# Short convolution on quarters of the TensorE array's rows, with a new written-out order, in a fused long-convolution and SwiGLU block

## The chip, the cores and the metric

The kernel runs on one core of a Trainium2 chip. The metric is the device time of one execution in microseconds (us); less is better. "The trace" is one execution recorded by the hardware profiler, "the profile" the page made from it. Engines: PE is TensorE (PEld its weight loads), DVE is VectorE, ACT is ScalarE, POOL is GpSimd, SP is SyncE, here only a queue that issues DMAs.

## The reference, cut to what matters

Sequence S = 2048, width D = 640, FFN width 1728, all bfloat16.

```python
x = A_q
n = layernorm(x)
kshift[t] = sum over i in 0..3 of k[t-i] * shift_k[:, i]     # short convolution, four taps per channel
kv = kshift * v
y = causal long convolution of kv with ssm_k (length 2048), by FFT
y = y + kv * ssm_D
h = x + n * y
out = h + (silu(layernorm(h) @ w_gate) * (layernorm(h) @ w_up)) @ w_down
```

## The kernel before, in words

**Blocks and stages.** The sequence is cut into NB = 4 blocks of 512 tokens. Token t of a block sits in partition t // 4, row r = t % 4, so a block is a tile of 128 partitions by 4 x 640. The FFT is done by matmuls with constant cosine and sine tables: `WF` forward and `WI` back, both loaded from HBM. For each block j there are these stages, in the names that the planner gives them:

- `k`: k is turned so that channels lie on partitions, in the tile `T` (block 0 by PE transposes, blocks 1 to 3 by transposing DMAs in `load_rows`). The short convolution runs on PE in `by_halves` (line 745), and ACT or DVE take the result out of PSUM and multiply it by v (lines 763, 764, 766). That gives kv.
- `X` and `G`: spectra of kv and of the filter (`spectrum`, `transform`, `forward`: matmuls on line 400, evictions on lines 389 and 392). `g_turned` first turns the filter block, by PE transposes (line 498) and evictions (line 500), or, for blocks in `GTURN`, by one ACT copy (line 484) and four transposing DMAs (line 488).
- `h` and `m`: DVE combines filter spectra of two blocks and multiplies and adds spectra (lines 544 to 567, 865, 893, 894). Block j needs j + 1 products. Some of the additions are given to DMAs that add into SBUF (line 292).
- `i`: the inverse transform (DVE sums on lines 979 to 1016, matmuls on line 1036), then for each of four rows the gate `n * y`, its row sum and the residual (`h1`, lines 1060 and 1074; block 0 on lines 1047 and 1050), then squares for the second layernorm (ACT, line 905) and the normalisation.
- `t`: the normalised rows are scaled (lines 960, 963) and turned, block 0 by PE (lines 1096, 1098), the others by four transposing DMAs (line 1089).
- `f`: the FFN of the block, 135 matmuls of 512 columns (line 1260) and 112 of the down projection (line 1153), with ACT and DVE between.

So block j's FFN can start when its `t` stage is complete; block j + 1's `k` to `t` stages run beside block j's FFN. What comes before the FFN of block 0 is called the prologue below.

**Sums in the spectrum.** `transform` makes a spectrum from sums over even and odd rows. In the way called "sub" each of four output groups takes two accumulations of four matmuls (two rows, two column halves), and DVE makes the upper half with one subtraction of 128 x 2560. In the way called "four" (listed in `SUM`) it uses a further symmetry: half of the matmuls, the same number of evictions, and on DVE two differences of 128 x 1280 (line 464) and two sums of 128 x 2560 (lines 468, 471).

**Short convolution.** `pairs` holds, for each tap and each group of 128 channels, a diagonal matrix folded to 64 columns, built once on DVE (line 1424). A matmul takes 64 of the array's 128 rows: the weights are a window of `T` (64 channels by 128 tokens), the moving operand up to four taps by 64 columns. The two halves of the rows write to two PSUM banks. The five channel groups are done in three goes of 2, 2 and 1, each with one PSUM slot of two banks.

**Order.** A planner, `Plan`, numbers every piece of work (`plan.add`) with the engine it runs on, the buffers it needs and an assumed duration. `schedule` then emits the pieces in the order of the list `ORDER`, so this list fixes the sequence on every engine and DMA queue. A negative number picks a piece's alternative: DVE instead of ACT, a POOL-issued DMA instead of one from SP, or an adding DMA instead of a DVE addition. The assumed durations are used only to make the list; at run time the engines wait on semaphores. There are four PSUM slots (`ps`) of two banks each, shared by all stages, and 13 SBUF slots (`big`).

At the start PE multiplies ones (`spin`, line 1410, counts in `WARMUP` and `SPINS`) so that its clock is up, while the first loads come in.

Of the kernel before, what the change touches and what calls it, by code (L numbers as in the profile page):

```python
# [44 lines left out]
GTURN = (3,)  # L45
KTURN = (1, 2, 3)
SUM = {'X2': 'four', 'X3': 'four', 'i2': 'four', 'i3': 'four', 'G3': 'four'}
# [3 lines left out]
WARMUP = (18, 16, 16)  # L51
SPINS = (2, 2)
MERGE = ()
WIDE = ()
H1ACT = ()
# [17 lines left out]
TAPROWS = True  # L73
TWONS = 640
# [146 lines left out]
def kernel(ctx: ExitStack, tc: tile.TileContext, A_q, A_k, A_v, A_shift_k, A_ssm_k, A_ssm_D, B_x,  # L221
# [93 lines left out]
    if TAPROWS:  # L315
        T = fixed([P, KT * TW], BF16, "T")
        ident2 = fixed([P, P // 2], BF16, "ident2")
        pairs = fixed([P, 4 * KT, P // 2], BF16, "pairs")

        def tk():  # L320
            return ap(T).rearrange("p (c t) -> p c t", c=KT)

        def tk0():
            return ap(T)[:, 0:KT * R * (P + 1)].rearrange("p (c r t) -> p c r t", c=KT, r=R)
        TOKENS = tuple((a, r) for a in range(R) for r in range(R))
    else:
        diag = new("diag") if TWOTAPS else fixed([P, KT * 4, P], BF16, "diag")
# [342 lines left out]
    def kv_of(j, kT, before, v, behind=None):  # L670

        if TAPROWS:
            if j == 0:
                dve(60, lambda: nc.vector.memset(tk0()[:, :, :, 0:1], 0.0), [], [of_t("K0")])
            kv = new("t4")
            by_halves(j, kv, v, behind)
            return kv
# [932 lines left out]
```

## Time and profile before

| | |
|---|---|
| median of 3 runs | 255.96 us (255.7 to 256.19) |
| the profiled execution | 256.9 us, of which the span of instructions is 254.8 us |
| PE busy | 247.1 us, 97% of the span |
| DVE busy | 193.7 us, 76% |
| ACT busy | 171.0 us, 67% |
| POOL busy | 61.2 us, 24% |
| granted TensorE clock | 1.0 |
| DMA | 42.80 MB, mean 168 GB/s |

The profiled execution took 0.9 us more than the median. Busy time of PE counts overlapping matmuls as busy throughout, so its share is read together with the chain of waits: the list of instructions, followed back from the last one, of which each released the next.

### The profile page before, as it was taken

What the parts mean: (1) busy time and instruction counts of PE and PEld (TensorE: products, weight loads), DVE (VectorE), ACT (ScalarE), POOL (GpSimd) and SP (SyncE); (2) the same over time, 40 slices, a digit from 0 to 9 for tenths busy, and PEclk for the clock granted to TensorE, in tenths of its full rate; (3) what the DMA queues carried; (4) which work ended last, traced back from release to release, by engine and by line L of the source; (5) the groups of instructions that cost most, each with busy time, mean ns of one, the idle gap of its engine ahead of it and who ended that gap; (6) DMA issues with size and microseconds to landing.
All of it is one profiled execution on the core that took longest, in us unless ns stands there. A gap on an engine that the chain in (4) does not pass through costs nothing.

```text
span 254.8 us, 4493 instructions
## 1 busy us (share of the span) xinstructions
PE 247.1 (97%) x1758; PEld 146.8 (58%) x1758; DVE 193.7 (76%) x256; ACT 171.0 (67%) x295; POOL 61.2 (24%) x72
## 2 busy tenths in 40 slices
PE   8889999999999999999999999999999999999995
PEld 8756776644445776654564576544447754444663
DVE  0879999999999999999999999999999100020322
ACT  2789989987989964877796965645697244653400
POOL 2203240012560400541415203309900042000000
PEclk9999999999999999999999999999999999999999
DMA  5999999999996797999977877997770476000003
GB/s 183 391 345 152 371 287 219 330 190 174 166 256 135 174 155 168 192 223 176 289 170 104 207 134 166 253 195 124 152 215 1 93 103 115 0 3 0 0 0 105
DMA packets 54591, 42.80 MB, mean 168 GB/s; under 512 B 25557, under 2 KB 48730, under 8 KB 54570
## 3 DMA queue, kind: packets, MB, share of 16 engines
q1 hardware_dynamic: 47664, 28.25, 44.3%
q0 software_dynamic: 6896, 14.26, 30.6%
q8 instruction: 14, 0.23, 0.4%
q14 instruction: 7, 0.06, 0.1%
q10 hardware_dynamic: 10, 0.01, 0.0%
HBM read 23.99 MB, written 4.59 MB: 112 GB/s over the span
## 4 chain that ended last, share of the span: by engine, by line
PE 83%; ACT 7%; DMA 4%; DVE 2%; SPq 1%; issue 1%; DVEq 0%
PE ps L1260 46%; PE ps L1153 24%; PE ps L400 6%; DMA WF<-const_wf 4%; PE ps L1036 4%; PE ps L745 3%; ACT big L389 3%; ACT S L389 2%; DVE big L1050 1%; ACT big L500 1%; ACT big L1098 1%; ACT row L905 1%; DVE row L1047 1%; SPq L362 0%; PE ps L498 0%
## 5 line engine op out<-in xcount | busy, mean ns | idle before, releaser
L1260 PE MATMUL ps<-big,big 128*128 128x512 bf16 x540 | 119.4, 379 | 0.0
L1260 PEld LDWEIGHTS <-big 128*128 128x128 bf16 x540 | 52.7, 98 | 61.1 <-issue 0.2
L1153 PE MATMUL ps<-wd,tT 128*128 128x320 bf16 (+2 forms) x416 | 58.4, 299 | 0.0
L1153 PEld LDWEIGHTS <-tT 128*128 128x128 bf16 x416 | 40.1, 98 | 17.0 <-issue 1.3
L400 PE MATMUL ps<-big,WF 128*128 128x320 bf16 x224 | 35.9, 298 | 3.2 <-DMA WF<-const_wf 1.6
L1252 ACT ACTIVATE tT<-ps 128x1024 bf16<-128x1024 f32 x24 | 24.5, 1023 | 17.5 <-PE ps L1260 17.4
L893 DVE TENSOR_TENSOR big<-S,S 128x2560 bf16<-128x2560 bf16 x24 | 34.9, 1487 | 0.1
L1254 DVE TENSOR_TENSOR tT<-tT,co 128x2048 bf16<-128x2048 bf16 x12 | 14.6, 1222 | 25.0 <-ACT co L1250 25.0
L1250 ACT CAST co<-ps 128x1024 bf16<-128x1024 f32 x24 | 23.9, 1012 | 12.8 <-PE ps L1260 11.3
L400 PEld LDWEIGHTS <-WF 128*128 128x128 bf16 x224 | 21.5, 97 | 14.6 <-issue 3.5
L292 POOL DMA_DIRECT2D S<-big x13 | 15.2, 1173 | 55.7 <-DVE big L865 24.7
L894 DVE TENSOR_TENSOR S<-S,big 128x2560 bf16<-128x2560 bf16 x16 | 23.7, 1487 | 0.1
L905 ACT ACTIVATE row<-big 128x640 bf16<-128x640 bf16 x32 | 23.5, 735 | 0.5 <-DVE big L1050 0.2
L963 ACT ACTIVATE row<-big,sm 128x640 bf16<-128x640 bf16 x20 | 17.7, 921 | 6.8 <-DVE sm L941 6.8
L1189 POOL DMA_DIRECT2D out_dram<-row x12 | 13.1, 1231 | 22.4 <-ACT row L1188 22.1
L389 ACT ACTIVATE big<-ps 128x640 bf16<-128x640 f32 (+1 forms) x29 | 16.8, 625 | 0.9 <-PE ps L400 0.9
L1188 ACT CAST row<-ps 128x640 bf16<-128x640 f32 x12 | 7.7, 699 | 13.8 <-PE ps L1153 12.3
L389 ACT CAST S<-ps 128x640 bf16<-128x640 f32 (+1 forms) x26 | 14.7, 623 | 1.1 <-PE ps L400 1.1
L952 ACT ACTIVATE row<-big 128x640 bf16<-128x640 bf16 x16 | 11.9, 741 | 1.4 <-DMA big<-in_A_q_dram 1.4
L865 DVE TENSOR_TENSOR S<-S,S 128x2560 bf16<-128x2560 bf16 (+1 forms) x10 | 12.1, 1220 | 0.0
L865 DVE TENSOR_TENSOR big<-S,S 128x2560 bf16<-128x2560 bf16 (+1 forms) x10 | 12.0, 1220 | 0.0
L1036 PEld LDWEIGHTS <-WI 128*128 128x128 bf16 x96 | 9.2, 98 | 4.8 <-issue 0.2
(99 smaller groups left out, 265.0 us busy)
## 6 DMA issues: line engine op xcount, KB each, us to landing
S<-big POOLq DMA_DIRECT2D x11, 640.0 KB, 6.2
big<-in_B_w_gate_dram SPq DMA_DIRECT2D x13, 320.0 KB, 5.6
big<-in_B_w_up_dram SPq DMA_DIRECT2D x12, 320.0 KB, 6.2
big<-in_A_ssm_k_dram SPq DMA_DIRECT2D x4, 640.0 KB, 9.6
big<-in_A_q_dram SPq DMA_DIRECT2D x4, 640.0 KB, 5.0
big<-in_A_v_dram SPq DMA_DIRECT2D x4, 640.0 KB, 8.3
wd<-in_B_w_down_dram SPq DMA_DIRECT2D x1, 2080.0 KB, 9.4
out_dram<-big SPq DMA_DIRECT2D x3, 640.0 KB, 5.0
```

What stands on the lines that cost most here:

```text
L389: (lambda: nc.scalar.activation(dst(), src(), ACT.Copy, scale=2.0)) if twice else (lambda: nc.scalar.copy(dst(), src())),
L400: nc.tensor.matmul(ap(ps)[:, h, 0:NH], w, ap(src)[:, r, h * NH:(h + 1) * NH], start=(first and i == 0), stop=(last and i == len(rs) - 1), ...
L865: return lambda: f(*(x() for x in args))
L893: dve(1490, lambda b=b, xs=xs, hs=hs: nc.vector.tensor_mul(flat2(b), X.part(xs), H.part(hs)), [X.at(xs), H.at(hs)], [b], [A.b])
L894: dve(1490, lambda b=b, dst=dst, f=f: f(A.part(dst), A.part(dst), flat2(b)), [b], [A.at(dst)])
L905: act(825, lambda r=r, junk=junk: nc.scalar.activation(ap(junk), ap(x)[:, r, :], ACT.Square, scale=D ** -0.5, accum_out=sm(s, 1)[:, r:r + ...
L963: nc.scalar.activation(ap(row), ap(x)[:, r, :], ACT.Identity, bias=sm(s, 5)[:, r:r + 1], scale=sm(s, 4)[:, r:r + 1])
L1036: nc.tensor.matmul(ap(ps)[:, w, 0:NH], m, src[:, w * NH:(w + 1) * NH], start=(i == 0), stop=(i == len(terms) - 1))
L1153: nc.tensor.matmul(to, t, w, skip_group_check=True, **flags)
L1250: act(1010, lambda ps=ps: nc.scalar.copy(ap(co)[:, at:at + 2, :], ap(ps)), src, [(co, gi % 2)])
L1252: act(1010, lambda ps=ps: nc.scalar.activation(ap(tT)[:, c:c + 2, :], ap(ps), ACT.Silu), src, [done(range(c, c + 2), ROWS)])
L1260: nc.tensor.matmul(ap(ps)[:, i, :], ap(w)[:, k, off:off + P], ap(hT)[:, k, :], start=(k == 0), stop=(k == KT - 1))
```

## The change

- `TAPQ`: the short convolution uses quarters of the array's rows (`by_quarters` instead of `by_halves`). A matmul takes 32 rows, and `pairs` is folded once more, to 32 columns. There are four matmuls side by side where there were two, each with half the columns, and they write to four PSUM banks, so two slots. The channel groups are done in two goes, of 4 and of 1. The takes out of PSUM are split accordingly.
- `H1ACT = (1, 2, 3)`: in blocks 1 to 3 a row of the inverse may be copied out of PSUM by ACT, multiplied on DVE in SBUF, and summed by ACT; as the alternative stands the old single DVE instruction. `ORDER` chooses row by row.
- `SUM` no longer lists `X2`, so the spectrum of block 2's kv is made in the way "sub".
- `GTURN = (2, 3)`: block 2's filter is turned by transposing DMAs.
- `WARMUP` and `SPINS` change: more spins ahead of the first work, two groups of four fewer.
- `ORDER` is a new list. In it, among other things, the first loads from SP go in the order filter, k, v, `WF`, x (before: k, filter, x, v, `WF`).

```diff
-GTURN = (3,)
+GTURN = (2, 3)
-SUM = {'X2': 'four', 'X3': 'four', 'i2': 'four', 'i3': 'four', 'G3': 'four'}
+SUM = {'X3': 'four', 'i2': 'four', 'i3': 'four', 'G3': 'four'}
-WARMUP = (18, 16, 16)
-SPINS = (2, 2)
+WARMUP = (26, 24, 16)
+SPINS = (0, 2)
-H1ACT = ()
+H1ACT = (1, 2, 3)
+TAPQ = True
 ORDER = [
...
-        pairs = fixed([P, 4 * KT, P // 2], BF16, "pairs")
+        pairs = fixed([P, 4 * KT, P // (4 if TAPQ else 2)], BF16, "pairs")
...
-            by_halves(j, kv, v, behind)
+            (by_quarters if TAPQ else by_halves)(j, kv, v, behind)
...
+    def by_quarters(j, kv, v, behind):
+        H4 = P // 4
...
+        for cs in (range(KT - 1), range(KT - 1, KT)):
+            n = len(cs)
+            pss = [conv_ps(), conv_ps()]
+
+            def mm(cs=cs, pss=pss):
+                for at in (0, 1, -1, 2, -2, 3, -3):
+                    r0, r1 = max(0, at), min(R - 1, R - 1 + at)
+                    for c in cs:
+                        for b in range(4):
+                            rows = slice(b * H4, b * H4 + H4)
+                            nc.tensor.matmul(ap(pss[b // 2])[:, b % 2, 0:len(cs) * R * H4].rearrange("p (r c e) -> p r c e", r=R, e=H4)[:, r0:r1 + 1, c - cs[0], :], window(rows, c, at),
+                                             ap(pairs).rearrange("p (t c) e -> p t c e", c=KT)[rows, r0 - at:r1 - at + 1, c, :],
+                                             start=(at == 0), stop=(abs(at) > 1), skip_group_check=True, tile_position=(b * H4, 0))
+            op = pe(300 * n + 190, mm, [of_t("halo", *TOKENS, *(() if j else FIRSTS)), pairs], pss, [kv], 258)
...
+            for half, ps in enumerate(pss):
...
+                if n > 1:
+                    def straight(dst=dst, src=src, ps=ps, half=half, cs=cs):
+                        nc.vector.tensor_mul(dst(), src(ps), by(cs, half).rearrange("p r c (b e) -> p r c b e", b=2))
+                    op = plan.add("act", 1010, lambda dst=dst, src=src, ps=ps: nc.scalar.copy(dst(), src(ps)), [ps, v], parts, (), ("dve", 1230, straight))
+                    op.rest = (dve(690, lambda half=half, cs=cs: nc.vector.tensor_mul(to(cs, half), to(cs, half), by(cs, half)), [v], parts),)
+                else:
...
+                    act(430, lambda flat=flat: nc.scalar.copy(*flat()), [ps, v], parts)
+                    plan.ops[-1].other = ("dve", 490, lambda flat=flat: nc.vector.tensor_copy(*flat()))
...
+            if n == 1:
+                dve(420, lambda: nc.vector.tensor_mul(ap(kv)[:, :, (KT - 1) * P:], ap(kv)[:, :, (KT - 1) * P:], rd(v)[:, :, (KT - 1) * P:]), [v, *whole], [*whole, (kv, "w2")])
...
-        dve(1480, lambda: nc.vector.tensor_mul(ap(pairs), ap(ident2).unsqueeze(1).broadcast_to([P, 4 * KT, P // 2]), ap(taps).unsqueeze(2).broadcast_to([P, 4 * KT, P // 2])), [ident2, taps], [pairs])
+        PW = P // (4 if TAPQ else 2)
+        if TAPQ:
+            plan.add("pool", 350, lambda: nc.gpsimd.tensor_tensor(ap(ident2)[:, 0:PW], ap(ident2)[:, 0:PW], ap(ident2)[:, PW:2 * PW], op=ALU.add), [ident2], [ident2])
+        dve(810 if TAPQ else 1480, lambda: nc.vector.tensor_mul(ap(pairs), ap(ident2)[:, 0:PW].unsqueeze(1).broadcast_to([P, 4 * KT, PW]), ap(taps).unsqueeze(2).broadcast_to([P, 4 * KT, PW])), [ident2, taps], [pairs])
```

The part of `inverse` that `H1ACT` switches on stood in the kernel already:

```python
if plan.block in H1ACT:
    y, junk = new("row"), new("row")
    op = act(700, lambda ps=ps, y=y: nc.scalar.copy(two(ap(y)), half(ap(ps))), [ps, t], [y, t, (s, ("s", r))])
    op.other = ("dve", 820, h1)
    op.rest = (dve(490, lambda t=t, y=y: nc.vector.tensor_mul(ap(t), ap(t), ap(y)), [y], [t]),
               act(820, lambda r=r, t=t, s=s, junk=junk: nc.scalar.activation(
                   ap(junk), ap(t), ACT.Identity, accum_out=sm(s, 0)[:, r:r + 1]), [t], [junk, (s, ("s", r))]))
```

More of the change, by code (lines that the diff above doesn't have):

```diff
@@ L401, in mm @@
                                      start=(first and i == 0), stop=(last and i == len(rs) - 1), skip_group_check=True)
-        pe(136 * len(ws) * len(rs), mm, [(src, x) for r in rs for x in (r, f"{r}w", f"{r}n")] + [(src, f"w{i}") for i in range(ws[0], ws[-1] + 2)] + [WF] + ([(m, "f")] if m else []) + ([] if first else [ps]), [ps], holds)
+        pe(136 * len(ws) * len(rs), mm, [(src, x) for r in rs for x in (r, f"{r}w", f"{r}n")] + [(src, f"w{i}") for i in range(0 if TAPQ else ws[0], ws[-1] + 2)] + [WF] + ([(m, "f")] if m else []) + ([] if first else [ps]), [ps], holds)
     def wide(n, ws):
@@ L766, in by_halves, with window, to, by @@
             op.rest = (dve(690 if n > 1 else 420, lambda cols=cols: nc.vector.tensor_mul(cols(ap(kv)), cols(ap(kv)), cols(rd(v))), [v], [(kv, f"w{i}")]),)
+    def by_quarters(j, kv, v, behind):
+        H4 = P // 4
+        def window(rows, c, at):
+            if j:
+                return tk()[rows, c, PAD + at:PAD + at + BLK - 3:R]
+            return tk0()[rows, c, at % R, at >= 0:P + (at >= 0)]
+        def to(cs, half):
+            return ap(kv)[:, :, cs[0] * P:(cs[-1] + 1) * P].rearrange("p r (c f) -> p r c f", f=P)[..., half * H2:(half + 1) * H2]
+        def by(cs, half):
+            return rd(v)[:, :, cs[0] * P:(cs[-1] + 1) * P].rearrange("p r (c f) -> p r c f", f=P)[..., half * H2:(half + 1) * H2]
+        for cs in (range(KT - 1), range(KT - 1, KT)):
[11 more added lines that the diff above has]
+            op = pe(300 * n + 190, mm, [of_t("halo", *TOKENS, *(() if j else FIRSTS)), pairs], pss, [kv], 258)
+            if behind:
+                op.deps.add(behind)
+            def src(ps, n=n):
+                return ap(ps)[:, :, 0:n * R * H4].rearrange("p b (r c e) -> p r c b e", r=R, e=H4)
+            whole = []
+            for half, ps in enumerate(pss):
+                def dst(half=half, cs=cs):
+                    return to(cs, half).rearrange("p r c (b e) -> p r c b e", b=2)
+                parts = [(kv, f"w{half}")] if n > 1 else [(kv, f"v{half}")]
+                if n > 1:
[4 more added lines that the diff above has]
+                else:
+                    def flat(ps=ps, half=half):
+                        return ap(kv)[:, :, (KT - 1) * P + half * H2:(KT - 1) * P + (half + 1) * H2].rearrange("p r (b e) -> p r b e", b=2), ap(ps)[:, :, 0:R * H4].rearrange("p b (r e) -> p r b e", r=R)
+                    act(430, lambda flat=flat: nc.scalar.copy(*flat()), [ps, v], parts)
+                    plan.ops[-1].other = ("dve", 490, lambda flat=flat: nc.vector.tensor_copy(*flat()))
+                    whole += parts
+            if n == 1:
+                dve(420, lambda: nc.vector.tensor_mul(ap(kv)[:, :, (KT - 1) * P:], ap(kv)[:, :, (KT - 1) * P:], rd(v)[:, :, (KT - 1) * P:]), [v, *whole], [*whole, (kv, "w2")])
@@ L1467 @@
     load(P * R * 4 * P * 2, 4096, lambda: nc.sync.dma_start(out=ap(WF), in_=wf_h.ap()), [WF])
+    plan.ops[-1].ns += 900
     first("Lg0")
     g = load_g(0)
+    plan.ops[-1].ns += 400
     first("Lm")
```

77 rows, old and new, of the table ORDER are left out of this document.

## The prediction

> **What bounds the kernel now.** I read three views in this order: the page's head and its chain of waits, the busy time by stage, and the chain piece by piece.
>
> ```profile
> PE 83%; ACT 7%; DMA 4%; DVE 2%; SPq 1%; issue 1%; DVEq 0%
> ```
>
> PE holds 83% of the chain. The stages show where it doesn't (start and end in us, length, then busy time and instructions of each engine):
>
> ```profile
> 21.00:43.90 22.90, 21.83 (x225) 15.98 (x223) 22.80 (x34) 21.74 (x45) 4.97 (x3) 1.00 1.12 269
> 51.30:110.06 58.76, 58.62 (x402) 33.97 (x401) 57.11 (x65) 47.99 (x85) 17.86 (x22) 1.00 0.91 179
> 110.06:160.96 50.90, 50.90 (x348) 28.79 (x347) 50.34 (x60) 37.27 (x61) 14.23 (x15) 1.00 0.89 186
> 160.96:207.44 46.48, 46.48 (x267) 25.35 (x265) 36.45 (x50) 27.18 (x42) 15.34 (x16) 1.00 0.68 141
> ```
>
> The columns after the length are PE, PEld, DVE, ACT, POOL. In the prologue (to 51.3) DVE is as full as PE, 22.80 of 22.90. From 51.3 on PE has no gap to speak of, but DVE has none either until block 3's inverse is done: 57.11 of 58.76, 50.34 of 50.90. So PE sets the time after 51.3, with DVE just behind. A microsecond taken from PE there is worth a microsecond; one taken from DVE alone is worth nothing; in the prologue it is the other way round. Pieces of the chain (start, length, what, count):
>
> ```profile
> 51.28 27.05 PE ps L1260 x125
> 78.33 1.03 PE ps L745 x28
> ...
> 82.72 3.26 PE ps L1036 x24
> 85.98 0.57 PE ps L745 x14
> ...
> 100.45 1.03 PE ps L745 x28
> 101.48 1.19 PE ps L1153 x8
> 102.67 0.23 PE ps L1410 x4
> ...
> 103.34 0.84 DVE S L392
> ...
> 110.06 15.11 PE ps L1260 x70
> ```
>
> The FFNs start at 51.28, 110.06, about 161 and 207.44. Block 2's convolution costs PE 1.03 + 0.57 + 1.03 = 2.63 us.
>
> **The change part by part.**
>
> *Convolution on quarters.* Stretches of one go of 28 matmuls, this line alone (x counts what runs into the stretch too):
>
> ```profile
> 78.51:78.84 0.33, 0.33 (x12) 0.33 (x10) 1.00 0.95 171
> 78.84:79.06 0.22, 0.22 (x12) 0.22 (x10) 1.00 1.09 198
> 79.06:79.29 0.23, 0.23 (x14) 0.19 (x10) 1.00 1.04 189
> 10.20:12.30 2.10, 1.95 (x56) 1.79 (x56) 1.00 1.00 408
> ```
>
> In the first four pairs of 192 columns start (the other four of the 12 run in): 0.083 us a pair. In the second four pairs of 128 columns: 0.056. In the third four pairs of 64 columns start, in some 0.13 us of it: 0.033 a pair. So the two matmuls of a pair go side by side: 28 matmuls have 2 x 2048 columns, which at the FFN's 512 columns in 27.05 / 125 = 0.216 us would take 1.73 us one after the other, and they take 1.03. By columns 64 would cost 0.027, so 0.033 is near a floor for a step. With quarters a channel group has seven steps of four matmuls: one of 128 columns (0.056), two of 96 (0.042), two of 64 and two of 32 (0.033 each). Sum 0.27, five groups 1.36 us. A go costs more than its steps: the old steps are 0.108 for 256 columns (by the FFN's rate) + 2 x 0.083 + 2 x 0.056 + 2 x 0.033 = 0.45 a group, and 2.63 less five of them is 0.37 for three goes, 0.12 each. With two goes: 1.36 + 0.25 = 1.6; I take 1.7. The upper bound is that loads and matmuls can't be fed faster than in that densest spot, eight matmuls in 0.13 us, 0.0165 each: 140 would take 2.3 + 0.25 = 2.55, no gain; or, far worse, no faster than over the longest dense run shown, 56 in 1.95 us or 0.035 each: 4.9. I take 1.7 because the pair is the nearest row, and in it doubling the row groups costs no visible time. Gain 0.9 a block. Blocks 2 and 3 lie on the path: **-1.9**. Block 0 ends ahead of `WF` and block 1 in the prologue, where DVE sets the pace: 0. The takes out of PSUM go from three to four a block; that adds one short ACT instruction, beside other work. Building `pairs` halves on DVE ahead of `WF`: 0.
>
> *X2 in the way "sub".* PE gets 16 more matmuls of 320 columns at 3.26 / 24 = 0.136: **+2.2** on PE's path. DVE loses two differences and one of two big sums:
>
> ```profile
> L464 DVE TENSOR_TENSOR big<-S,big 128x1280 bf16<-128x1280 bf16 x2 | 1.6, 822 | 0.0
> L471 DVE TENSOR_TENSOR S<-S,big 128x2560 bf16<-128x2560 bf16 x2 | 3.0, 1492 | 0.1
> L484 ACT COPY big<-big 128x2560 bf16<-128x2560 bf16 x1 | 2.6, 2572 | 0.0
> L389 ACT CAST big<-ps 128x640 bf16<-128x640 f32 x8 | 5.3, 708 | 0.0
> L1060 DVE SCALAR_TENSOR_TENSOR row<-row,ps 128x640 bf16<-128x640 bf16 x12 | 9.7, 818 | 0.0
> ```
>
> 2 x 0.82 + 1.49 = 3.1 us, taken from an engine that is not first there: worth 0 itself. But at 102.67 PE spins (0.23) and at 103.34 waits 0.84 for DVE's take of X2. The new order has X2's matmuls among the last of block 0's FFN and no spin there: **-1.0**. Next late is ACT: three copies, seven takes of X2, one scaling, a copy and five takes of G3 before the FFN finds a PSUM slot, 17 in all. A take lasts 0.71, but in a row they overlap:
>
> ```profile
> 105.43 1.29 ACT L389 CAST big<-ps 128x640 bf16<-128x640 f32 x2
> ```
>
> Two last 1.29, so they follow 0.59 apart: 17 x 0.59 = 10.0 us, against 64 x 0.136 + 2 x 1.1 = 10.9 of PE work in that place. It is covered by 0.9 us; without overlap it would be 12.0, 1.1 too long.
>
> *Block 2's filter by transfers.* 20 transposes leave PE, in the prologue where PE isn't the bound, and four evictions of a take's size (0.71) leave ACT for one copy of 2.57 (line 484, block 3's): about 0. The four transfers join SP's queue, by the row on line 1089 below some 1.2 us of issue each. Behind them stand the first FFN's weights, which in before are issued from 23 us on for use at 51 and later: covered.
>
> *Rows copied by ACT.* In the new order six of the twelve rows go this way (two, three, one in blocks 1, 2, 3). DVE loses the 0.82 of line 1060 less a multiply, so 0 to 4.9 us in all, and isn't first: 0. ACT gains a copy and a summing pass of a take's size, 1.4 each and 8.5 in all, over three stages that leave it 10.8, 13.6 and 19.3 us free: 0. If that cover goes, a row's chain grows by about 1 us ahead of the transfers of `t`. Those decide in one place:
>
> ```profile
> 103.33 1.21 SPq L1089 DMA_TRANSPOSE big<-row  x1
> ```
>
> ```profile
> DMA to landing us min/median/max: 2.6/2.6/6.2
> ```
>
> The second row is over all twelve transfers of line 1089. The last of block 1's is issued at 103.33, and with the longest 6.2 us to land that is 109.5, just ahead of the FFN at 110.06. In the new order its last scaling still stands behind seven takes of X2: I put **+0.3** there, between -0.2 and +2.
>
> *The prologue.* First what the loads release, then DVE:
>
> ```profile
> 9.09 1.73 DVE L500 COPY big<-ps 128x640 bf16<-128x640 bf16 x4 [0.27 <-PE ps L498]
> 9.64 0.74 ACT L952 ACTIVATE row<-big 128x640 bf16<-128x640 bf16 x1 [1.35 <-DMA big<-in_A_q_dram]
> 11.43 2.96 DVE L763 TENSOR_TENSOR big<-ps,big 128x512 bf16<-128x512 f32 x3 [0.23 <-DMA big<-in_A_v_dram]
> 13.80 0.45 PE L400 MATMUL ps<-big,WF 128*128 128x320 bf16 x2 [1.63 <-DMA WF<-const_wf]
> 20.99 0.82 DVE L865 TENSOR_TENSOR big<-S,S 128x1280 bf16<-128x1280 bf16 x1
> 43.91 0.17 DVE L924 TENSOR_SCALAR sm<-sm 128x4 f32<-128x4 f32 x1
> 46.98 1.49 DVE L435 TENSOR_TENSOR S<-big,S 128x2560 bf16<-128x2560 bf16 x1
> 48.39 0.44 DVE L960 TENSOR_SCALAR row<-big,sm 128x640 bf16<-128x640 bf16 x1
> ```
>
> PE waits for `WF` until 13.80; v, of x's size, came 1.8 us after x. With x behind `WF`, spectra start some 1.7 us sooner, at about 12.1, and DVE's first product moves from 20.99 to 19.3. Between that and the normalisation at 43.91 the new order gives DVE five more takes out of PSUM (four of block 1's filter, one of G0), at 1.73 / 4 = 0.43 each 2.1 us, so 44.3. After it, G2's subtraction no longer stands ahead of the fourth scaling (48.39 - 46.98 = 1.4 less), but two evictions do (0.9 more): 48.2 instead of 48.39. From there the FFN took until 51.28, with ACT's last eviction behind takes of X1; ACT is freed of two evictions, for which I take 0.3. Together **-0.5** for the FFN's start. Lower end: the 1.7, the 0.5 and the 0.3 all stay, -2.5. Upper end: (d) below.
>
> The FFNs of blocks 2 and 3 and the end are unchanged.
>
> **Sum**: -1.9 + 2.2 - 1.0 + 0.3 - 0.5 = -0.9 us against the profiled execution's 256.9, which gives 256.0. That execution stands 0.9 above the median of 255.96, so 255.1 as a median: 0.3% faster.
>
> **The rivals.** What a measurement here can tell from no change is about 0.2%, 0.5 us.
>
> (a) *The prologue keeps its whole shift.* ACT has less to do after `WF` and DVE's extra takes fill gaps: -2.5 instead of -0.5, so **253.1**. Against it: 22.80 of 22.90 on DVE leaves no gaps.
>
> (b) *Quarters bring nothing*: each matmul at 0.0165, 2.55 a block. Two blocks lose 1.7: **256.8**.
>
> (c) *Quarters are slower, because single matmuls can't follow each other fast enough.* A block now issues 140 with a load each, a go of 112 without a pause, where the longest dense run shown is 56. Between 0.0165 and 0.035 I take the middle, 0.026: 3.6 us a block, 1.95 worse than forecast, on two blocks: **259.0**. It decides from 0.017 a matmul on, where the forecast's gain is gone.
>
> The Trainium skill has a rule that speaks for (c): "TensorE: Matmul & The Clock Gate", section "Wait — 56ns, not 53.3ns?", puts the start-to-start time at no less than about 25 ns however small the matmul. By it 140 matmuls would need 3.5 us and the kernel about 258.7. Here the trace disagrees in part: eight matmuls within 0.13 us are 16.5 ns each, so if there is such a floor it holds for a row group by itself; no row shows four groups.
>
> (d) *The prologue gets slower.*
>
> ```profile
> 12.26 9.19 SPq L588 DMA_TRANSPOSE T<-in_A_k_dram  x4
> big<-in_A_v_dram SPq DMA_DIRECT2D x4, 640.0 KB, 8.3
> ```
>
> Block 1's k transposes hold SP for 9.19 us. In before its filter and v are issued ahead of them; in the new order the filter stands behind the first and v behind all four. v would be issued at about 22 and land 8.3 us later, at 30.3, and ACT's take of block 1's convolution, which waits for v, would be due at about 29 by what stands ahead of it there (22 half-width takes, eight passes of the first layernorm, the copy of 2.57). Everything behind it on ACT (G1's takes, then block 0's squares) moves by 1.3 to 3, which turns -0.5 into +1.5 in the middle: **257.1**. Slower from a delay of 1 us on.
>
> **How the numbers follow.** Chances: forecast 0.42, (a) 0.20, (b) 0.10, (c) 0.12, (d) 0.16. The forecast's own range is 254.0 to 256.3: of its chance 0.25 is faster by more than 0.5 us, 0.11 within, 0.06 slower. (a) is faster. Of (b) 0.02 and of (d) 0.03 lie within, of (d) 0.01 is faster, the rest and (c) slower. Sum: faster 0.46, same 0.16, slower 0.38. The range runs from 252.6, a little past (a), to 259.0, the middle of (c).
>
> **What would show it.** Right: a block's 140 convolution matmuls take 1.6 to 1.8 us of the chain; `WF` releases PE at about 12.1; the FFNs start near 50.8, 110.1, 160.2 and 206.6; no wait of more than 0.5 us between X2 and the second FFN. Wrong: steps of four matmuls that take over 0.06 us; PE waiting at the second FFN for a transfer of `t` or for ACT's takes; ACT waiting for v of block 1 near 29; DVE reaching block 0's normalisation after 45.

## The result, and the profile after

Slower: median 266.78 us (265.95 to 266.9, 4 runs) against 256.07 on the same chip (255.7 to 257.03); ratio 1.0405, interval 1.037 to 1.0441. Forecast were 255.1, and 252.6 to 259.0 as the range. The profiled execution has a span of 263.9 us against 254.8, some 9 us more. The medians are 10.7 us apart: the profiled execution of the changed kernel, 265.95 us, was its shortest, and that of the kernel before stood 0.9 us above its median.

The FFNs start at 56.6, 115.94, 169.48 and 216.1 in the chain of waits, where 51.28, 110.06, 160.96 and 207.44 stood. So the prologue lost 5.3 us, the stage of the first FFN 0.6, that of the second 2.6, the rest 0.5. The stages of the changed kernel (columns as in the prediction's table):

```profile
0.00:56.60 56.60, 46.83 (x631) 34.05 (x632) 42.85 (x81) 41.27 (x83) 7.16 (x17) 0.97 0.89 255
56.60:115.94 59.34, 59.10 (x481) 34.50 (x483) 57.01 (x63) 51.33 (x93) 25.48 (x21) 1.00 0.90 170
115.94:169.50 53.56, 51.31 (x414) 28.45 (x417) 49.70 (x59) 36.50 (x59) 16.36 (x17) 0.97 0.87 185
```

PE's busy time in the prologue is what it was (46.83; 46.87 in the first 51.3 us before), so PE stood still 5.3 us longer. The last three columns are the granted clock, the DMA share and GB/s; the clock is 0.97 in the two stages that lost most, and was 1.00 in the four of before that the prediction shows. The timeline of PE (start, length, what, count, in brackets the idle time ahead and its releaser) shows where it stood:

```profile
10.56 1.22 PE L793 MATMUL ps<-pairs,T 32*128 32x128 bf16 x105
14.18 0.42 PE L793 MATMUL ps<-pairs,T 32*128 32x64 bf16 x35 [2.40 <-issue]
14.53 0.72 PE L402 MATMUL ps<-big,WF 128*128 128x320 bf16 x4
30.69 1.38 PE L793 MATMUL ps<-pairs,T 32*128 32x128 bf16 x114 [0.17 <-DVE big L502]
32.96 0.42 PE L793 MATMUL ps<-pairs,T 32*128 32x128 bf16 x22 [0.89 <-DVE big L502]
35.19 0.21 PE L793 MATMUL ps<-pairs,T 32*128 32x32 bf16 x4 [1.80 <-issue]
134.36 1.30 PE L793 MATMUL ps<-pairs,T 32*128 32x128 bf16 x112 [1.65 <-ACT tT L1305]
```

Block 0's convolution stops in its middle for 2.40 us and block 1's four matmuls from its end for 1.80, both with "issue" as the reason: nothing that the profile records released them. Block 3's starts 1.65 late. And twice the granted clock is half, for 3.41 us each, as the busy times of these two stretches show:

```profile
16.31:19.72 3.41, 3.41 (x15) 1.96 (x14) 2.13 (x5) 2.58 (x8) 0.00 (x0) 0.50 0.77 145
135.78:139.19 3.41, 3.19 (x10) 1.51 (x10) 1.97 (x3) 2.16 (x3) 0.74 (x1) 0.50 1.21 246
```

The matmuls themselves ran as fast as forecast or faster. The chain has them (start, length, what):

```profile
92.25 1.22 PE ps L793 x111
134.38 1.28 PE ps L793 x101
```

111 matmuls in 1.22 us are 11 ns each, where 16.5 was the densest spot before.

### The profile page after: what moved, and what is told of

Same layout as the page of the kernel before. It is cut to its first block, busy times and chain, and to the rows that moved or that the text cites. A ratio compares the mean times of both kernels' runs of the same rounds, so it can differ in the third digit from the quotient of the medians.

```text
span 263.9 us, 5065 instructions
## 1 busy us (share of the span) xinstructions
PE 247.7 (94%) x2027; PEld 145.7 (55%) x2042; DVE 192.0 (73%) x258; ACT 176.4 (67%) x308; POOL 68.0 (26%) x73
## 4 chain that ended last, share of the span: by engine, by line
PE 72%; DVE 15%; ACT 6%; issue 4%; DMA 2%; DVEq 0%; ACTq 0%
PE ps L1313 40%; PE ps L1206 17%; PE ps L402 6%; PE ps L1463 3%; PE ps L1089 2%; DMA big<-row 2%; DVE S L918 2%; PE ps L793 2%; DVE S L437 1%; DVE big L1103 1%; DVE big L946 1%; ACT tT L1305 1%; DVE row L1100 1%; ACT big L391 1%; DVE tT L1307 1%
## 5 line engine op out<-in xcount | busy, mean ns | idle before, releaser
L1206 PE MATMUL ps<-wd,tT 128*128 128x320 bf16 (+2 forms) x416 | 59.7, 299 | 0.0
L402 PE MATMUL ps<-big,WF 128*128 128x320 bf16 x240 | 39.7, 308 | 2.7 <-ACT big L391 1.4
L402 PEld LDWEIGHTS <-WF 128*128 128x128 bf16 x240 | 23.8, 100 | 15.2 <-issue 4.8
L294 POOL DMA_DIRECT2D S<-big x11 | 13.0, 1226 | 50.6 <-DVE big L918 29.1
L947 DVE TENSOR_TENSOR S<-S,big 128x2560 bf16<-128x2560 bf16 x17 | 25.1, 1485 | 0.1
L1242 POOL DMA_DIRECT2D out_dram<-row x12 | 13.9, 1350 | 34.3 <-ACT row L1241 34.3
L391 ACT CAST S<-ps 128x640 bf16<-128x640 f32 (+1 forms) x29 | 16.1, 607 | 3.6 <-PE ps L402 3.5
L1016 ACT ACTIVATE row<-big,sm 128x640 bf16<-128x640 bf16 x17 | 15.0, 919 | 0.9 <-DVE sm L994 0.9
L1325 DVE TENSOR_TENSOR tT<-tT,co 128x512 bf16<-128x512 bf16 x4 | 1.7, 421 | 18.5 <-ACT co L1324 18.5
L793 PE MATMUL ps<-pairs,T 32*128 32x64 bf16 (+3 forms) x560 | 7.4, 195 | 7.0 <-issue 4.2
```

The lines of the kernel that those rows point to most:

```text
L391: (lambda: nc.scalar.activation(dst(), src(), ACT.Copy, scale=2.0)) if twice else (lambda: nc.scalar.copy(dst(), src())),
L402: nc.tensor.matmul(ap(ps)[:, h, 0:NH], w, ap(src)[:, r, h * NH:(h + 1) * NH], start=(first and i == 0), stop=(last and i == len(rs) - 1), ...
L947: dve(1490, lambda b=b, dst=dst, f=f: f(A.part(dst), A.part(dst), flat2(b)), [b], [A.at(dst)])
L1016: nc.scalar.activation(ap(row), ap(x)[:, r, :], ACT.Identity, bias=sm(s, 5)[:, r:r + 1], scale=sm(s, 4)[:, r:r + 1])
L1206: nc.tensor.matmul(to, t, w, skip_group_check=True, **flags)
```

## The experiments

**Theory T1.** "issue" in the middle of a run of equal matmuls could be a lack of instructions. The view of the DMA queues lists one of the kind "instruction" with its packets, MB and share, in before:

```profile
q8 instruction: 14, 0.23, 0.4%
```

and in the changed kernel, the whole span and the stretch from 11.70 to 13.00, within the first stop:

```profile
q8 instruction: 16, 0.26, 0.4%
...
q8 instruction: 1, 0.02, 4.9%
```

0.23 MB in 14 packets are 16 KB each. The convolutions have 280 matmuls and as many weight loads more, some 560 instructions, and two more packets came: as if a packet were a piece of the list, of some 256 to 280 instructions. I took 256.

T1: if PE uses up a piece of 256 instructions before the next piece is there, it stands. R1: the stops belong to the matmuls (a slot, a transfer, the filter). To tell them apart I only moved the convolution along the list, with small matmuls ahead of it:

```
-    spun = spin(WARMUP[1])
+    spun = spin(WARMUP[1], 58)          # 24 in shift48
     # in spin: 58 times matmul(warm[:, 0, 0:8], ones, ones[:, 0:8])
```

> 58 matmuls of 8 columns (116 instructions of TensorE) are added behind the second group of spins; nothing else differs from the changed kernel. T1 (TensorE's instructions come in pieces of 256 that are asked for late; it stands where it uses 256 of them in less than some 4.5 us): the piece's border moves from the 104th matmul of block 0's convolution to about the 48th, with the spins and transposes ahead of it as time to fetch; the stops of 2.40 us in block 0's convolution and of 1.80 us in block 1's go to under 0.3 us each, the first FFN starts at 52.5 to 54.5 instead of 56.6, and the median falls by 2 to 4 us to 263-265. R1 (a wait that belongs to the matmuls themselves: a PSUM slot, the filter, a transfer): the stops stay behind the 104th and the 136th matmul, the time stays within 0.7 us of the changed kernel's or is longer by the added matmuls' 1 us.

> The same with 24 small matmuls, 48 instructions. T1: block 0's convolution now stops behind its 82nd matmul instead of its 104th, and for some 1.4 us instead of 2.4, because the piece is asked for about 1.1 us earlier against the convolution's start; block 1's stop of 1.80 moves from behind the 136th to behind the 113th matmul, where its second go waits anyway. The first FFN starts at 54 to 56, the median falls by 0.5 to 2 us. R1: both stops stay where they are, at their lengths.

Measured: shift48 262.99 us, ratio 1.0234 (1.0174 to 1.0295); shift116 267.34, 1.0376 (1.0314 to 1.0438). The timeline of PE in shift48:

```profile
10.59 1.04 PE L793 MATMUL ps<-pairs,T 32*128 32x128 bf16 x81
12.38 0.62 PE L793 MATMUL ps<-pairs,T 32*128 32x64 bf16 x59 [0.75 <-issue]
30.12 0.46 PE L793 MATMUL ps<-pairs,T 32*128 32x128 bf16 x28 [1.24 <-DVE big L502]
```

and in shift116:

```profile
11.86 0.98 PE L793 MATMUL ps<-pairs,T 32*128 32x96 bf16 x93 [0.17 <-issue]
87.19 1.15 PE L793 MATMUL ps<-pairs,T 32*128 32x128 bf16 x96
90.10 0.32 PE L793 MATMUL ps<-pairs,T 32*128 32x32 bf16 x16 [1.77 <-issue]
```

The stop moved from behind the 105th matmul to the 81st, as T1 said, and was 0.75 long (1.4 expected); in block 1 it fell together with the wait of 0.89 between the goes, 1.24 in all; in shift116 it was down to 0.17 in block 0 and gone from block 1, and a new one of 1.77 stood in block 2, where there had been none and where T1's forecast had named none. Counted from the list's start, the stop is always at one place. The busy times up to the two stops, whose x counts are the PE and PEld instructions so far, in the changed kernel:

```profile
0.00:11.78 11.78, 10.87 (x223) 10.13 (x224) 4.14 (x11) 4.54 (x7) 2.22 (x11) 1.00 0.76 281
0.00:33.38 33.38, 26.49 (x478) 20.29 (x479) 21.60 (x40) 21.84 (x48) 6.01 (x16) 0.95 0.82 266
```

and in shift48:

```profile
0.00:11.62 11.62, 10.70 (x223) 9.97 (x224) 3.96 (x11) 4.54 (x7) 2.22 (x11) 1.00 0.76 278
0.00:28.88 28.88, 24.41 (x478) 19.27 (x479) 19.96 (x38) 20.21 (x47) 5.18 (x15) 1.00 0.90 281
```

447 and 957 instructions in both kernels, 510 apart: two pieces, less the few records that a trace lacks. The new stop of shift116 fits the same count:

```profile
0.00:88.33 88.33, 81.95 (x989) 52.49 (x989) 77.64 (x109) 73.27 (x139) 27.17 (x29) 1.00 0.95 238
```

1978 instructions are 1021 more than 957, four pieces of 255. T1 stands, R1 falls. From the matmul that enters a piece to the first one of the piece after it, PE needed 5.1 us (9.04 to 14.18 in the changed kernel, 7.29 to 12.38 in shift48), 4.4 and 5.1 in block 1, 5.5 in shift116's block 2. (The matmul that enters a piece is found by counting 255 records back from the stop.) In shift48 the first FFN starts at 51.63 on the timeline (56.43 in the changed kernel): with most of the two stops and all of the half clock behind them gone, 4.8 of the prologue's 5.3 us are back. In shift116 it starts at 51.43, earlier than the 52.5 to 54.5 expected, but the kernel as a whole gained nothing, and the 263 to 265 expected was missed: its block 2 got the new stop, and block 3's convolution waited 5.58 us. That leads to the second loss.

**The late start of block 3's convolution.** The view names ACT's SiLU as the releaser, which ran from 133.34 to 134.38, so T2 was that a row copied by ACT holds that SiLU back. One row was given back to DVE, in the order:

```
-    ... 643, 505, 559, ...
+    ... 643, -506, 559, ...             # row 3 of block 2 in one DVE instruction
```

> Of the six inverse rows that ScalarE copies in the changed kernel, one (row 3 of block 2) goes back to VectorE's single instruction. T2 (ScalarE stands at this copy, waiting for the inverse's matmuls, with a SiLU behind it whose PSUM slot block 3's convolution needs; the pause lets the clock fall): TensorE's pause of 1.65 us ahead of block 3's convolution goes to 0.5 or less, the granted clock stays at 1.00 after it, the stage from the second FFN to the third goes from 53.6 to 50.5-51.8 us, the median falls by 1.8 to 3. R2 (the clock falls because of the burst of 112 matmuls in 1.2 us): the pause goes and the clock still falls to about half behind the convolution; gain 0.5 to 1.5. R3 (VectorE's chain of block 2's inverse and the last transfer of t set this stage): VectorE has 0.33 us more to do, gain 0 to 0.5 or a loss.

267.43 us, 1.0415 (1.037 to 1.046): no gain. In the profiled execution, the longest of the four with 270.88, the pause was there, 3.86 us long. T2 fell. Here, and in shift116, the chain of waits shows another releaser, in row3dve a transfer from 130.00 to 139.31, with PE starting at 139.44. In shift116 (start, length, what):

```profile
118.40 5.71 SPq L590
124.16 11.02 DMA T<-in_A_k_dram
135.31 1.95 PE ps L793 x87
```

These are the transfers that turn block 3's k. In the changed kernel SP issues the last three of them here, by its timeline:

```profile
113.61 1.22 SPq L590 DMA_TRANSPOSE T<-in_A_k_dram  x1
114.93 0.53 SPq L1184 DMA_DIRECT2D big<-in_B_w_up_dram  x1
120.95 0.37 SPq L1184 DMA_DIRECT2D big<-in_B_w_gate_dram  x1
121.37 8.57 SPq L590 DMA_TRANSPOSE T<-in_A_k_dram  x2
```

SP stands at a weight load until 120.95 (the view of waits names a DVE instruction, line 947, that releases its buffer, for 5.4 us), and k's last two transfers are behind it; they land at 133.69 and 134.23, and PE starts at 134.36, 0.13 behind, as in shift116 (135.18 and 135.31) and row3dve (139.31 and 139.44). The ACT instruction that the view named ended at 134.38, no sooner than PE's start, so these times alone can't tell the two apart. In before the last two were issued at 105.96 and 108.30 and landed at 111.3 and 113.6. The next two kernels change the place of the two, alone and with shift48's matmuls:

```
-    ..., 607, 556, ..., 604, ..., 606, ...
+    ..., 607, 604, 606, 556, ...
```

> The changed kernel with one edit of the order: the last two transfers that turn block 3's k (line 590) stand directly behind the second, ahead of two weight loads on SyncE's queue; in the changed kernel the second of these loads waits until 120.95 for a buffer, and the transfers behind it are issued at 121.37 and 126.92 and land at 133.69 and 134.23. T3 (TensorE's pause of 1.65 us ahead of block 3's convolution waits for these transfers, whatever the view names, and the half clock of 3.41 us follows from the pause): the transfers are issued by 118 and land by 124, the pause goes to under 0.3 us, the clock stays at 1.00 there, the stage from the second to the third FFN goes from 53.65 to 49.9-51.0, the median falls by 2.6 to 4, to about 263.3. R2 (the burst of matmuls takes the clock down): the pause goes, the clock still falls; 265. R3 (VectorE's chain sets this stage): within 0.7 of 266.8.

> The edit of the order above together with the 24 small matmuls of the run shift48. T1 and T3 add up: the first FFN starts near 51.6 as in shift48, the stage from the second to the third FFN is 49.9 to 51.0, the median is 258.5 to 260 and the profiled span near 255.5; the four times lie closer together than shift48's 260.9 to 266.5, since that spread came from the late transfers. If T3 is wrong it stays at 262-263.

k3early: 265.38, 1.0333 (1.0292 to 1.0374). both: 260.29 (257.75 to 264.82), 1.0126 (1.0076 to 1.0175). In both, profiled at a span of 255.8, SP's and PE's timelines are as T3 says:

```profile
109.52 3.90 SPq L592 DMA_TRANSPOSE T<-in_A_k_dram  x3
128.25 1.29 PE L795 MATMUL ps<-pairs,T 32*128 32x128 bf16 x112
129.47 1.25 PE L1315 MATMUL ps<-big,big 128*128 128x512 bf16 x4
```

No wait, the clock at 1.00 through the whole span, and the stage is 49.92 us. In before the stage took 50.91, so with the transfers early it is 0.99 shorter, and the pause was theirs. The burst of 112 matmuls doesn't take the clock down; that the pause ahead of it did fits all four kernels that had one (changed, shift48, shift116, row3dve). k3early alone gained less than expected (stage 52.63): PE waited twice for weights instead, by its timeline:

```profile
132.65 2.33 PE L1315 MATMUL ps<-big,big 128*128 128x512 bf16 x10 [1.25 <-DMA big<-in_B_w_gate_dram]
137.99 1.25 PE L1315 MATMUL ps<-big,big 128*128 128x512 bf16 x4 [1.24 <-DMA big<-in_B_w_up_dram]
```

That the spread of the times would go was wrong: they lie between 257.75 and 261.46, one at 264.82. The kernel still had stops of 1.15 and 1.23 us in the prologue.

**Is it the quarters or the new order?** The kernel before, in its own order, with quarters in place of halves (each block's three goes become two that take two PSUM slots, moved behind until four slots sufficed):

> The kernel before with the convolution on quarters alone: its own order of work, sums, spins and loads; the goes of a block are two instead of three, each with two PSUM slots, so the goes of blocks 1 and 2 stand a little later in the order. T1 and the 11 ns a matmul of the changed kernel: each of blocks 2 and 3 gives back 0.95 us, no pause in the convolution above 0.5 us, so 256.1 - 1.9 = 254.2, and up to 255.5 with waits for the second PSUM slot. R4 (two slots at once cost more than the faster matmuls bring, wherever they stand): pauses of over 1 us ahead of the goes, 256.0 to 259.

270.09, 1.0538 (1.0511 to 1.0565), the slowest so far. The prologue lost 6.9 us with the old order of loads too, with stops of 2.09 and 1.96 us behind 447 and 957 records again, so they come with the quarters; the second of them stands ahead of transposes of the filter, behind the convolution, so a stop isn't tied to the convolution's matmuls. My expectation named no stop above 0.5, which did not follow from T1: its list has the border within block 0's go. The rest of the loss, 4.7 us in the stage of the first FFN and 1.8 in the next, is waits around the moved goes; it doesn't price the quarters.

**Fewer instructions instead of a moved border.** Blocks 0 and 1 on halves again, in the changed kernel's goes, slots and takes, with k3early's order and no matmul added; then all four blocks:

```
+    for at in (0, 1, -1, 2, -2, 3, -3) if j < 2 else ():        # halves_all: j < 4
+        for c in cs:
+            for b in range(2):     # 64 rows, 70 matmuls a block; slot b, bank (c - cs[0]) // 2
```

> The changed kernel with the order of k3early, and with blocks 0 and 1 convolved on halves of the rows in the same goes, slots and takes (70 matmuls a block instead of 140); blocks 2 and 3 stay on quarters. No matmul is added ahead. T1: the borders of 256 instructions now fall outside both convolutions of the prologue, so no pause inside block 0's convolution, and in block 1's only the one of 0.9 us between its goes, which was there in every run; no half clock in the prologue; the first FFN starts at 51.2 to 52.7 although these two convolutions take 2.6 us each instead of 1.2 to 1.7; stages behind it 59.4, 50-51.5, 46.5, 47.9; median 257 to 260. R1 (the pauses belong to the new order of the prologue or to the two slots of a go): pauses of over 1 us stay in both, the first FFN starts at 55 to 58.

> The same with all four blocks on halves. It prices the quarters where they lie on TensorE's path: if the 0.95 us a block count there, the stages from the first to the second and from the second to the third FFN are each 0.8 to 1.0 us longer than in halves01, and the median 1.5 to 2 us. If waits for transfers or for VectorE take the gain up, the difference is under 0.7.

halves01: 257.80 (12 runs), 1.0033 (1.0006 to 1.0059). halves_all: 259.52, 1.0095 (1.0062 to 1.0127). The timeline of PE in halves01:

```profile
11.39 2.40 PE L797 MATMUL ps<-pairs,T 64*128 64x256 bf16 x70
28.30 2.08 PE L797 MATMUL ps<-pairs,T 64*128 64x256 bf16 x57 [0.16 <-DVE big L504]
30.57 0.61 PE L797 MATMUL ps<-pairs,T 64*128 64x256 bf16 x13 [0.19 <-DVE big L504]
```

and the stretch that was at half clock:

```profile
16.31:19.72 3.41, 3.05 (x21) 1.90 (x20) 3.41 (x8) 3.41 (x12) 0.00 (x0) 1.00 1.01 248
```

The slower convolution has no stop (the wait of 0.9 in block 1 is 0.19), no half clock, and the kernel is 7.6 us faster than k3early. It differs from k3early in this alone and in a table of taps that is 64 columns wide and sliced for the quarters, built without the second POOL addition. Not all of the 7.6 is the prologue's: by the table below the first FFN starts 5.5 us sooner, and the stage of the second FFN is 2.4 shorter, where k3early's two waits for weights, 1.25 and 1.24, don't come up. All but one of its runs lie between 257.37 and 258.73. The difference of the medians to halves_all, 1.72 us, is the quarters' worth where PE is the bound, and the two stages show it as 0.87 and 0.80. The stages, by the first FFN matmul on the timeline (the medians come from several batches of runs; the kernel before had 256.0 to 256.9 in them):

| kernel | 1st FFN starts | to 2nd | to 3rd | to 4th | median |
|---|---|---|---|---|---|
| before | 51.19 | 58.70 | 50.91 | 46.48 | 256.07 |
| changed | 56.43 | 59.40 | 53.65 | 46.46 | 266.78 |
| shift48 | 51.63 | 59.41 | 53.36 | 46.47 | 262.99 |
| k3early | 57.81 | 59.40 | 52.63 | 46.47 | 265.38 |
| both | 51.87 | 59.56 | 49.92 | 46.47 | 260.29 |
| halves01 | 52.32 | 59.39 | 50.21 | 46.46 | 257.80 |
| halves_all | 51.64 | 60.26 | 51.01 | 46.46 | 259.52 |

**What the supply gives with few other transfers.** In the changed kernel, behind the last matmul:

```
+    for _ in range(512):
+        nc.tensor.matmul(place["ps"][0][:, 0, 0:8], ones, ones[:, 0:8], start=True, stop=True)
```

> The changed kernel with 512 matmuls of 8 columns (1024 instructions of TensorE) behind its last matmul, where no other transfers run. It measures the supply of instructions alone. T1 with a delay that belongs to the fetch itself: the matmuls run in groups of about 128 with pauses, 256 instructions in 4 to 5.2 us, 16 to 21 us in all. T1 with a delay made by the other transfers: 256 instructions in about 2 us, 8 to 9 us in all. R1 (no such limit): 512 matmuls one behind the other at 25 to 30 ns, 13 to 15 us and no pauses.

PE's timeline, and then the queue's packets over the whole span:

```profile
263.89 13.54 PE L1640 MATMUL ps<-const-bfloat16-1.0 128*128 128x8 bf16 x512
```

```profile
q8 instruction: 20, 0.33, 0.5%
```

1024 instructions more, four pieces more, and no stop: 25 ns a matmul until 267.82, 26.7 from there on, where the granted clock was 0.50 (0.65 over the whole stretch); 256 instructions in 3.2 to 3.4 us. So a piece doesn't always need 5.1 us. The time came out as the expectation's R1 had it, 13 to 15 us and no pauses; but no limit at all doesn't fit the stops above. Both T1 cases missed: the burst used a piece too slowly to find the limit, since a matmul on all rows didn't start more often than every 25 ns. In the prologue the piece's packet started 2.8 us after PE had entered the piece before it (9.04, 11.85), here 0.1 to 0.6 us for the first three, by the same count of records. At the stops a packet then took about 1.0 us, and PE went on 1.3 to 1.5 us after its end.

That the other transfers make the packet late is not shown. In block 2 of shift48 PE passed a piece in 3.7 us without a stop (87.40 to 91.08) at a DMA share of 1.03, with the packet 0.6 us behind; at the second stop of the changed kernel the DMA share was 0.81 while the packet was outstanding, and it came after 1.8. What decides how late a packet starts stays open.

**X2.** Last, halves01 with X2 back in the way "four":

```
-SUM = {'X3': 'four', ...
+SUM = {'X2': 'four', 'X3': 'four', ...   # its takes in the places of the old ones
```

> halves01 with X2 back in the way 'four' (16 matmuls of 320 columns fewer, 2.2 us of TensorE; two differences and a sum more on VectorE), its takes in the same places of the order. If the prediction's pricing of X2 holds (+2.2 for the matmuls, -1.0 for the wait and spin that they replaced), the stage from the first to the second FFN goes from 59.4 to 58.2 with a wait of some 1 us for VectorE's or ScalarE's part ahead of the second FFN, and the median from 257.8 to 256.6, at the kernel before's 256.9. Rival: the wait for VectorE is as long as the matmuls saved, because the kernel before had its order made around it; the stage stays at 59.4 or grows, 257.8 to 259.

261.60, 1.0196 (1.0169 to 1.0223): the rival's way, and past its 259; the stage took 62.76 us where halves01 has 59.39. The view of waits, from 90 to 118 us (who waited for what, us in total, times, longest):

```profile
PE ps L1331 <- DMA big<-row: 1.8, 1, 1.8
PE ps L404 <- ACT S L393: 1.6, 3, 0.8
PE ps L404 <- DVE big L396: 1.5, 1, 1.5
```

4.9 us of waits, none of which halves01 has there, against 2.2 us of matmuls saved. It shows that in this order "sub" is the better way; it doesn't check the price of 1.0 for the wait by itself.

## Why the prediction was wrong

Point by point.

- *Rate of the quarters: right.* 1.7 us a block was forecast; in the chain block 2 took 0.45 + 1.22 and block 3 1.28 + 0.39, 1.67 each. On PE's path the two blocks gave 1.72 us (halves_all less halves01) for the -1.9. Rival (b) fell. Rival (c) had the right direction by luck: it priced a slower rate in blocks 2 and 3, and they ran at 11 ns; the loss lay in the stops of blocks 0 and 1, which it left out, and in block 3's late k. The floor of 25 ns that the Trainium skill's page "TensorE: Matmul & The Clock Gate" states (section "Wait — 56ns, not 53.3ns?") was met by matmuls on all rows (25 to 27 ns in burst_end) and not by four row groups.
- *"Block 0 ends ahead of `WF` and block 1 in the prologue, where DVE sets the pace: 0": this step failed, by about 4.8 us (what shift48 gave back).* I counted PE's time in the two blocks and not what PE's list needs in order to keep up, and put the rest at nothing. Two stops, 2.40 and 1.80 us, and half clock for 3.41, worth some 1.7 by estimate, stood ahead of DVE's work. The cover was gone as well: with `WF` early nothing was left behind which block 0 could end, and the first spectrum started at 14.53 behind the convolution instead of at 12.1.
- *The page that bore on it.* "Runtime: NRT & Kernel Launch", section "Instruction fetch mechanics", in the Trainium skill describes a list refilled in blocks of 256 instructions; the 510 between stops in the changed kernel agree. It holds the refill to be hidden behind the time that an instruction takes to issue; here it wasn't, with 105 matmuls and their loads in 1.22 us.
- *Prologue otherwise: -0.5 forecast, +0.2 to +1.1 found* (shift116, shift48, halves_all, both and halves01 start the first FFN between 51.43 and 52.32, before at 51.19; halves01 and halves_all have the slower convolution, shift48 and both keep parts of the stops). DVE is busy 43.11 us in halves01's prologue against 42.23 before; whether the rest is order or transfers stays open. Rival (d)'s late v was not seen: between 20 and 40 us ACT waits for no transfer in the changed kernel.
- *The stage of the first FFN: -0.95 + 2.2 - 1.0 + 0.3 = +0.55 forecast, +0.6 found.* The sum came out; that each of its parts did is not shown. The quarters' part is -0.87 by halves_all, so the rest is some +1.5, as forecast, but x2four could not split it into +2.2, -1.0 and +0.3.
- *The stage of the second FFN, for which the sum has block 3's share of the -1.9 and nothing else: failed, by 3.5 us* (-0.95 forecast, +2.6 found). I followed the moved transfers of block 2's filter and of `t`, and put those of block 3's k on the same queue at nothing without a reason, though the whole order was new. The last landed at 134.23 where before had 113.6, though the stage itself began only 5.9 us later, and PE's pause of 1.65 us and the half clock behind it, worth some 1.7 by estimate, make 3.35 of the 3.5. In both, where they are early, the stage is 0.99 shorter than before: the -0.95 itself was right.
- *"The FFNs of blocks 2 and 3 and the end are unchanged": nearly right.* From the third FFN's start to the fourth's are 46.46 us for 46.48; from there to the end 0.4 more, in halves01 too, and no run looks for the cause.
- *The ACT rows: 0 forecast.* row3dve shows no gain from undoing the one that stood ahead of the pause.

Stops and the late k together, with the half clock behind two of the three pauses, make the difference: taking away both (halves01) leaves 257.80, 1.0033 of before. The sum of -0.9 left all of them out, so the forecast failed on two terms that it had put at nothing, not on the rate that it worked out with the most care. A version faster than the kernel before was not found.

## What to carry to other kernels

When an edit makes matmuls smaller and more, count instructions as well as columns: find the places where 256 of them pass in less time than a piece of the list needs to arrive (4.4 to 5.5 us at the stops here), and either use fewer there or move the border, looking where the next border then falls: in shift116 it fell into block 2. When a whole order is replaced, compare the issue time of every transfer on the shared queue, not only of those the edit names. And check a named releaser against its own end and against landings: where two candidates end within 0.2 us of each other, as here, move one of them.

## What the runs showed of the hardware

- Four row groups started a matmul with its load every 11 ns (111 in 1.22 us); 512 matmuls of 8 columns on all rows every 25 ns at full clock and 26.7 at half.
- PE's instructions came in pieces of 256; with the convolutions in the prologue at four different places of the list the stops there came behind 447 and 957 records or not at all, and the one in shift116's block 2 behind 1978. At the stops the next piece was usable 4.4 to 5.5 us after the one before was entered, at DMA shares of 0.54 to 1.03; without a stop 3.7 us was enough once, at 1.03.
- A pause of PE of 1.65 or 2.40 us was followed by half clock for 3.41 us, which began 1.4 to 2.1 us after its end in the changed kernel; with one of 5.58 us in shift116 half clock lasted 6.83 us and began 1.4 us before its end; the 1.80 us in block 1 of the changed kernel brought none. The page "TensorE: Matmul & The Clock Gate" of the Trainium skill, in Part 1, gives windows of 3413 ns that run freely; the lengths agree.
- The places agree too: in the changed kernel the clock changed at 16.31, 19.72, 135.78 and 139.19, which is 1, 34 and 1 steps of 3.413 apart. With every trace here cut into such steps from its first clock record on, half clock began 15 times behind a step in which PE stood for 1.54 us or more (leaving out the last 2 us of a kernel). Two steps with as much, 1.81 in the changed kernel and 1.56 in quarters_only, had none behind them, and no step with less had, but for one: in burst_end half clock began at 267.82 behind matmuls of 8 columns without a gap. So a pause seems to count by how much of it falls into one step; no run moved a pause against the steps to test it.
